# Turning w1 as raw fp32, reading lower_bound as rows, one chunk per turn and a new order of two scans in a tuned HGRN + maxout kernel

## The chip, the cores and the metric

The kernel runs on one core of one Trainium2 chip. The metric is the device time of one execution in microseconds (us); lower is better. Times quoted as "median" are medians over several executions. The profile is one execution recorded by the hardware; its "span" is some 2 us shorter than the timed number of the same execution. Engines are written PE (matmul), PEld (its weight loads), DVE (vector), ACT (scalar), POOL (GpSimd) and SP (the engine that issues most DMAs).

## The reference

```python
def _attn_ref(x, f_logit, lower_bound):          # x, f_logit: [4, 6144, 256] fp32
    f = lower_bound + (1 - lower_bound) * sigmoid(f_logit)
    h = 0
    for t in range(S):
        h = f[:, t] * h + (1 - f[:, t]) * x[:, t]
        y[:, t] = h
    return y

def _moe_ref(x, w1, w2, w_out):                  # x = y as [24576, 256]; w1, w2: [256, 1024]
    return np.maximum(x @ w1, x @ w2) @ w_out    # w_out: [1024, 256]
```

The kernel writes max(h1, h2) as h1 + relu(h2 - h1). With om = 1 - lower_bound it scans y without its factor om and puts om on the weights instead: `wd` = om·(w2 - w1) gives h2 - h1 in one product (the *first layer*), and `w13` = om·(w1 @ w_out) carries h1 straight to the output. For `w13`, w1 has to be turned (transposed) on PE. The *second layer* adds relu(h2 - h1) @ w_out and y @ `w13`.

## The kernel before

Tokens come in blocks of 512. Block 0 is loaded in two halves, cast to fp16 and turned by PE, so that work can start early; blocks 1 to 3 come as three chunks of one block. Chunks of 1024 tokens (from chunk 4 on) *cross*: POOL's DMA writes them as fp16 into a scratch in HBM, and a transposing DMA brings them back turned. From block 4 on the kernel works in pairs of blocks; a pair has 16 *slots*, each with two 128x512 matmuls of the first layer and 8 or 9 128x128 matmuls of a scheme that does the second layer of the pair before with seven products instead of eight. That scheme needs sums of quarters (`sum1` to `sum4`, tiles `S`), which DVE makes, beside the recurrences (`scan00`, `scan01`, `scan10`, `scan11` of a pair: first or second block, first or second half of the channels).

The head, with the weights, before the change:

```python
    NG = 2
    NQ = FC // NG                                   # 4
    ...
    def fetch_w(g):                                 # halves of w1 and w2 in turn, 512 KB each
        cols = slice(g * DFF // NG, (g + 1) * DFF // NG)
        for w, src in ((w1n, moe_w1), (w2n, moe_w2)):
            nc.sync.dma_start(out=w[g][:], in_=src[:, cols].rearrange("(kc p) f -> p kc f", p=P))
    def scale_w1(g):  # ACT: w1s = om * w1n, fp32
    def half_w1(g, copy):  # w1h = fp16 of w1s
    def turn_w1(g):
        pt = ps_o.tile([P, NQ, KC, P], HALF, name="ps")
        for q in range(NQ):
            for kc in range(KC):
                nc.tensor.transpose(pt[:, q, kc, :], w1h[g][:, kc, q : NQ * P : NQ], ident[:])
        return pt
    ...
        nc.scalar.dma_start(out=lbc[:], in_=lower_bound.rearrange("(h p) -> p h", p=P))
        fetch_first(0); fetch_first(1)              # f and x of block 0, two halves
        for g in range(NG):
            fetch_w(g)
        pool_waits(w1n[0][:, 0, 0:1])
        nc.gpsimd.dma_start(out=wob...)             # w_out
        for c in range(1, 6):
            for s in range(2):
                fetch(c, s)
        ...
        for q in range(24):                         # warm PE
            nc.tensor.transpose(wt[:, 0, 0:P], ident[:], ident[:])
        scale_w1(0); half_w1(0, nc.scalar.copy); scale_w1(1)
        pt0 = turn_w1(0)
        for pair in range(2):
            make_wd(0, pair)
            for fc in range(2 * pair, 2 * pair + 2):
                first_layer(0, fc)
        half_w1(1, nc.vector.tensor_copy)
        pt1 = turn_w1(1)
        for pair in range(2):
            make_wd(1, pair)
            for fc in range(4 + 2 * pair, 6 + 2 * pair):
                first_layer(0, fc)
        keep_w1T(0, pt0); keep_w1T(1, pt1)
        steps = turn_steps(1)
        make_w13(0)                                 # first product with w_out
        turn(steps[:8])                             # block 1: needs fT of chunk 1
        ...
        cross(4, 5)
```

The loop over pairs, with DVE's work placed by a position in the pair (nine positions to a slot):

```python
            seq = [
                (27, scans[p]["scan10"]),
                (36, scans[p]["scan11"]),
                (112, lambda: sum3(p)),
            ]
            if more:
                seq += [(64, decay0), (66, drive0), (70, scan00), (84, scan01),   # of pair p + 1
                        (131, decay1), (133, drive1)]
            if not first:
                seq += [(9, sum1 of p - 1), (18, sum2 of p - 1), (50, sum4 of p - 1)]
            ...
                if slot == 2 and p + 3 < NPAIR:
                    cross(blocks[2 * p + 6][3])
```

(Lines are joined and cut for reading.)

## Time and profile before

| | before |
|---|---|
| median time, 3 runs | 379.66 us (379.19 to 379.68) |
| span of the profiled run | 377.7 us |
| first matmul of the first layer | 11.48 us |
| first `w13` product (needs w_out) | 15.68 us |
| last first-layer matmul | 362.88 us |

The lines of the page that matter are the span, the busy times, and the shares of the chain that ended last:

```profile
span 377.7 us, 9593 instructions
...
PE 367.9 (97%) x4136; PEld 279.8 (74%) x4136; DVE 338.7 (90%) x410; ACT 302.4 (80%) x410; POOL 35.6 (9%) x79
...
PE 94%; DVE 3%; DMA 1%; issue 0%; SPq 0%; ACT 0%; DVEq 0%
```

PE is busy 97% of the span and is 94% of the chain. A kernel like this can change in time only where PE waits, where PE runs work that it need not run, or where PE starts late. The view of waits has one line per pair of waiter and releaser; after the colon stand the total in us, the number of waits and the longest. These are two of the waits of PE:

```profile
PE ps L137 <- DVE nat L128: 2.8, 2, 2.1
...
PE dT L441 <- DVE r L230: 0.2, 1, 0.2
```

The first is in the head, where PE waits for the casts of block 0's halves. The second is the only wait between 11.5 and 370 us: 0.24 us at 62 us, for a scan.

For the comparison I cut both executions at the same five PE instructions: the first first-layer matmul, the first matmul of block 1's first layer, the first-layer matmul that follows PE's first six matmuls on a tile `S` (pair 3, near 60 us), and the last first-layer matmul. The columns are the stretch, its length, busy us and instructions of PE, PEld, DVE, ACT and POOL, the granted PE clock, the DMA share and GB/s:

```profile
0.00:11.48 11.48, 6.68 (x56) 5.38 (x56) 6.46 (x17) 6.80 (x11) 3.92 (x12) 1.00 0.81 276
11.48:22.62 11.14, 11.14 (x102) 8.48 (x103) 8.89 (x17) 7.75 (x11) 3.39 (x7) 1.00 1.22 234
22.62:58.62 36.00, 36.00 (x264) 25.47 (x263) 29.10 (x45) 27.34 (x33) 2.48 (x6) 1.00 0.93 201
58.62:362.88 304.26, 304.02 (x3551) 231.01 (x3549) 287.33 (x326) 255.78 (x349) 25.78 (x55) 1.00 0.99 204
362.88:377.70 14.82, 10.04 (x169) 9.48 (x167) 6.93 (x8) 4.69 (x8) 0.00 (x0) 0.95 0.41 143
```

From 11.48 to 58.62 us PE's busy time equals the stretch: it is full. (The column of the clock reads 1.00 in the first stretch too; it doesn't show that PE runs slowly until the trace's throttle record grants the full clock, at 11.0 us.) The timeline has a line per group of like instructions: start, busy us, engine, source line, operation and tiles, and in brackets the idle time before and what ended it. Five groups of the head:

```profile
4.22 0.43 DVE L128 CAST nat<-osb 128x512 f16<-128x512 f32 x1 [2.66 <-DMA osb<-in_f_logit_dram]
...
7.94 2.77 PE L696 MATMUL dT<-ident 128*128 128x128 f16 x24
...
10.50 0.86 PE L383 MATMUL ps<-ident,S 128*128 128x128 f16 x8
...
10.97 1.65 DVE L365 SCALAR_TENSOR_TENSOR wd<-r,om 128x256 f16<-128x256 f32 x4
...
11.48 2.10 PE L441 MATMUL dT<-r,wd 128*128 128x512 f16 x8
```

f of block 0 is cast at 4.22 us; 24 warming transposes fill PE from 7.94 us at 107 ns each while the recurrence of block 0 runs; eight fp16 turns of w1 follow, `wd` is made from 10.97 us, and the first layer starts at 11.48 us. In pair 3's first slots DVE's order is this:

```profile
56.68 1.48 DVE L506 TENSOR_TENSOR S<-r 128x2560 f16<-128x2560 f16 x1
...
58.08 1.48 DVE L506 TENSOR_TENSOR S<-r,S 128x2560 f16<-128x2560 f16 x1
...
58.29 0.50 PE L650 MATMUL ps<-t,S 128*128 128x128 f16 x6
...
59.48 2.45 DVE L230 TENSOR_TENSOR_SCAN r<-ff,r,v 128x512 f16<-128x512 f16 x2
...
61.99 0.38 PE L441 MATMUL dT<-r,wd 128*128 128x512 f16 x1 [0.24 <-DVE r L230]
```

`sum1` (the 1.48 us at 56.68) ends at 58.16 us, 0.13 us before PE's first six matmuls on it (58.29). `sum2` follows, then both scans of the second block in one group, and the wait of 0.24 us at the end is the first layer's, for those scans.

### The profile page before, as it was taken

The page shows a single profiled execution, that of the slowest core. Times are in us where ns is not written, and L with a number is a line of the kernel's source. Part 1 is how long each engine was busy: PE and PEld are TensorE (multiplying, and loading weights), DVE is VectorE, ACT ScalarE, POOL GpSimd, SP SyncE. Part 2 cuts the span into 40 slices and gives each one's busy share as a digit, 9 for nine tenths or more (in the row PEclk, how much of TensorE's full clock was granted, in tenths as well). Part 3 has the DMA queues.
Part 4 walks back from the last instruction along what each step waited for, and adds up shares of the span by engine and source line. Part 5 has one row for each costly group of instructions (what it writes and reads, how often), then busy time and mean ns, then how long its engine had stood idle before and what let it go on. Part 6 is the DMA issues. An engine that isn't in the chain of part 4 may idle for free.

```text
span 377.7 us, 9593 instructions
## 1 busy us (share of the span) xinstructions
PE 367.9 (97%) x4136; PEld 279.8 (74%) x4136; DVE 338.7 (90%) x410; ACT 302.4 (80%) x410; POOL 35.6 (9%) x79
## 2 busy tenths in 40 slices
PE   5999999999999999999999999999999999999994
PEld 3777767777777777777777777777777777777784
DVE  4796789999999999999999999999999999999772
ACT  5865897888888798888888887887988888889752
POOL 1500101110101101101201201011011001010000
PEclk9999999999999999999999999999999999999999
DMA  7996979998999999999999899999899899980223
GB/s 254 246 223 131 309 143 214 227 193 189 273 134 257 223 184 266 222 184 225 203 200 301 208 161 254 147 247 274 132 263 279 134 241 221 185 282 3 112 113 114
DMA packets 104813, 77.17 MB, mean 204 GB/s; under 512 B 93570, under 2 KB 95618, under 8 KB 104066
## 3 DMA queue, kind: packets, MB, share of 16 engines
q1 hardware_dynamic: 101538, 51.19, 60.5%
q0 software_dynamic: 2544, 25.17, 34.7%
q8 instruction: 32, 0.52, 0.6%
q10 hardware_dynamic: 688, 0.20, 0.2%
q14 instruction: 11, 0.09, 0.1%
HBM read 53.48 MB, written 48.23 MB: 269 GB/s over the span
## 4 chain that ended last, share of the span: by engine, by line
PE 94%; DVE 3%; DMA 1%; issue 0%; SPq 0%; ACT 0%; DVEq 0%
PE ps L650 44%; PE dT L441 43%; PE ps L487 5%; DMA osb<-in_x_dram 1%; DVE S L506 1%; PE ps L180 1%; DVE r L230 1%; DVE r L264 1%; PE ps L397 0%; DVE v L223 0%; DVE osb L568 0%; DVE osb L496 0%; PE ps L137 0%; DVE osb L589 0%; PE ps L383 0%
## 5 line engine op out<-in xcount | busy, mean ns | idle before, releaser
L449 ACT ACTIVATE r<-dT 128x1024 f16<-128x1024 f32 x192 | 195.9, 1023 | 53.4 <-PE dT L441 53.2
L441 PE MATMUL dT<-r,wd 128*128 128x512 f16 x768 | 225.5, 379 | 0.4 <-DVE r L230 0.2
L650 PEld LDWEIGHTS <-S 128*128 128x128 f16 x1760 | 115.5, 101 | 37.6 <-issue 0.5
L650 PEld LDWEIGHTS <-r 128*128 128x128 f16 x1320 | 90.9, 101 | 36.8 <-issue 0.2
L230 DVE TENSOR_TENSOR_SCAN r<-ff,r,v 128x512 f16<-128x512 f16 x88 | 108.2, 1269 | 0.8
L650 PE MATMUL ps<-t,S 128*128 128x128 f16 x1320 | 101.6, 219 | 0.0
L506 DVE TENSOR_TENSOR S<-r 128x2560 f16<-128x2560 f16 x44 | 65.3, 1485 | 14.5 <-ACT r L449 14.4
L441 PEld LDWEIGHTS <-wd 128*128 128x128 f16 x768 | 67.6, 113 | 5.2 <-DVE wd L365 1.2
L650 PE MATMUL ps<-wob,r 128*128 128x128 f16 x704 | 69.9, 219 | 0.0
L506 DVE TENSOR_TENSOR S<-r,S 128x2560 f16<-128x2560 f16 x44 | 64.8, 1473 | 0.0
L285 ACT ACTIVATE u<-fT 128x512 f16<-128x512 f16 x88 | 56.0, 637 | 1.3 <-DMA fT<-scr 1.3
L213 DVE TENSOR_SCALAR ff<-u,nom 128x512 f16<-128x512 f16 (+1 forms) x98 | 31.5, 344 | 8.5 <-ACT u L285 3.7
L650 PE MATMUL ps<-w,r 128*128 128x128 f16 x176 | 38.5, 219 | 0.0
L348 POOL CAST waited<-fT 128x1 f32<-128x1 f16 x21 | 8.8, 418 | 282.8 <-DMA fT<-scr 282.8
L650 PE MATMUL ps<-t,r 128*128 128x128 f16 x430 | 34.1, 219 | 0.1
L568 DVE TENSOR_TENSOR osb<-ps,sn 128x512 f32<-128x512 f32 x44 | 30.1, 683 | 3.2 <-PE ps L650 3.2
L650 PE MATMUL ps<-wob,S 128*128 128x128 f16 x352 | 32.6, 219 | 0.0
L223 DVE TENSOR_TENSOR v<-u,xT 128x1024 f16<-128x1024 f16 x44 | 30.0, 682 | 0.0
L556 ACT COPY sn<-ps 128x512 f32<-128x512 f32 x44 | 25.8, 587 | 2.4 <-PE ps L650 2.4
L566 ACT COPY osb<-ps 128x512 f32<-128x512 f32 x43 | 25.0, 582 | 0.8 <-PE ps L650 0.8
L487 PEld LDWEIGHTS <-r 128*128 128x128 f16 x160 | 16.0, 101 | 6.6
L650 PE MATMUL ps<-w,S 128*128 128x128 f16 x88 | 19.3, 219 | 0.0
(58 smaller groups left out, 131.9 us busy)
## 6 DMA issues: line engine op xcount, KB each, us to landing
out_dram<-osb SPq DMA_DIRECT2D x46, 512.0 KB, 3.8
scr<-in_f_logit_dram POOLq DMA_DIRECT2D x22, 512.0 KB, 7.9
scr<-in_x_dram POOLq DMA_DIRECT2D x22, 512.0 KB, 10.5
r<-in_moe_w_dram SPq DMA_DIRECT2D x4, 512.0 KB, 6.9
fT<-in_f_logit_dram POOLq DMA_DIRECT2D x3, 256.0 KB, 7.9
xT<-in_x_dram POOLq DMA_DIRECT2D x3, 256.0 KB, 8.5
out_dram<-osb SPq DMA_DIRECT2D x3, 256.0 KB, 2.6
osb<-in_f_logit_dram SPq DMA_DIRECT2D x2, 256.0 KB, 4.5
```

The lines of the kernel that those rows point to most:

```text
L213: nc.vector.tensor_scalar(out=ff[:, h, cols], in0=u[:, h, cols], scalar1=nom[:, h : h + 1], scalar2=1.0, op0=ALU.mult, op1=ALU.add,)
L223: nc.vector.tensor_tensor(out=like(v[:, :, cols], xT), in0=like(u[:, :, cols], xT), in1=xT, op=ALU.mult,)
L230: nc.vector.tensor_tensor_scan(out=y_of(j, h), data0=ff[:, h, o : o + TB], data1=v[:, h, o : o + TB], initial=0.0 if t0 == 0 else y_of(j - ...
L285: nc.scalar.activation(out=mids[p + NBLK, "u"][:, h, cols], in_=held[c, 0][:, h, cols], func=AF.Sigmoid, scale=-1.0,)
L441: nc.tensor.matmul(dT[:, fc % 2, :], lhsT=wd[:, kc, unit_cols(fc)], rhs=y_of(j, kc), start=(kc == 0), stop=(kc == KC - 1),)
L449: nc.scalar.activation(out=rts[j, k][:, g - 1 : g + 1, :].rearrange("p q (i m) -> p q i m", m=P), in_=dT[:].rearrange("p q (m i) -> p q i ...
L487: nc.tensor.matmul(ps[:, r, :], lhsT=left, rhs=right, start=(s == 0 and r == 0), stop=(s == n - 1 and r == 1), skip_group_check=True,)
L506: nc.vector.tensor_tensor(out=t[:], in0=a, in1=b, op=op)
L556: nc.scalar.copy(out=t[:], in_=bank[b][:])
L566: nc.scalar.copy(out=dst, in_=bank[b][:])
L568: nc.vector.tensor_tensor(out=dst, in0=bank[b][:], in1=snap[name][:], op=ALU.add)
L650: nc.tensor.matmul(bank[b][:, i, :], lhsT=a[:, k, cols], rhs=w, start=fresh, stop=after is not None, skip_group_check=True,)
```

## The change

The intent has four parts. (1) lower_bound is read as two contiguous rows and turned by PE, not as 256 separate values. (2) w1 is fetched whole before w2 and turned raw, in fp32, as it lands; its scale om goes on `w13` at the end, so the fp16 casts of w1 vanish and all turns stand ahead of the first layer. w2 comes in quarters. (3) Chunks cross one at a time, so chunk 4 no longer waits for chunk 5; in the loop a chunk is then asked for two pairs ahead instead of three. (4) In pairs 2 and 3 some scans and gates move ahead of the sums. The core of the diff:

```diff
-    def cross(*cs):
-        if len(cs) > 1:
-            nc.sync.dma_start(out=seen[:], in_=scratch[1][cs[-1] % NSCR][CH - 1 : CH, 0:16])
-        for c in cs:
+    def cross(c):
             ...
-    NG = 2
+    NG = 4
     def turn_w1(g):
-        pt = ps_o.tile([P, NQ, KC, P], HALF, name="ps")
+        pt = ps_o.tile([P, NQ, KC, P], FP32, name="ps")
         ...
-                    pt[:, q, kc, :], w1h[g][:, kc, q : NQ * P : NQ], ident[:]
+                    pt[:, q, kc, :], half_of(w1n, g)[:, kc, q : NQ * P : NQ], ident_f[:]
     def make_w13(kc):
-        nc.scalar.copy(out=w13[:, kc, :], in_=psw[:, 0, :])
+        nc.scalar.mul(w13[:, kc, :], psw[:, 0, :], om[:, kc : kc + 1])
     ...
-        nc.scalar.dma_start(out=lbc[:], in_=lower_bound.rearrange("(h p) -> p h", p=P))
+        nc.scalar.dma_start(out=lbr[:], in_=lower_bound.rearrange("(h p) -> h p", p=P))
+        for h in range(DFF // TB):
+            fetch_w(w1n[h], moe_w1, h * TB)
         for g in range(NG):
-            fetch_w(g)
+            fetch_w(w2n[g], moe_w2, g * NQ * P)
-        for c in range(1, 6):
+        for c in range(1, 5):
     ...
+        lbc = ps_d.tile([P, TB], FP32, name="dT")
+        nc.tensor.transpose(lbc[:, 0:KC], lbr[:], ident_f[0:KC, 0:KC])
     ...
-        for q in range(24):
-            nc.tensor.transpose(wt[:, 0, 0:P], ident[:], ident[:])
-        half_w1(0, nc.scalar.copy)          # ... and the rest of the old head, in halves
+        for g in range(NG):
+            for q in range(6):
+                nc.tensor.transpose(wt[:, 0, 0:P], ident[:], ident[:])
+            pts.append(turn_w1(g))
+        for g in range(NG):
+            make_wd(g)
+            for fc in range(NQ * g, NQ * (g + 1)):
+                first_layer(0, fc)
-        cross(4, 5)
+        cross(4)
     ...                                     # in the loop over pairs:
-                (27, scans[p]["scan10"]),
-                (36, scans[p]["scan11"]),
+                (12 if p == PAIR0 + 1 else 36, scans[p]["scan11"]),
+            if p != PAIR0 + 1:
+                seq.append((27, scans[p]["scan10"]))
+            if first:
+                seq.append((126, scans[p + 1]["scan10"]))
-                    (131, scans[p + 1]["decay1"]),
-                    (133, scans[p + 1]["drive1"]),
+                    (110 if first else 131, scans[p + 1]["decay1"]),
+                    (111 if first else 133, scans[p + 1]["drive1"]),
-            gates = {4: 0, 6: 1, 12: 2, 14: 3} if more else {}
+            gates = {4: 0, 6: 1, 10 if first else 12: 2, 12 if first else 14: 3}
-                if slot == 2 and p + 3 < NPAIR:
-                    cross(blocks[2 * p + 6][3])
+                if slot == 2 and p + 2 < NPAIR:
+                    cross(blocks[2 * p + 4][3])
```

Here PAIR0 is 2. So `scan10` of pair 3 runs at the end of pair 2, and `scan11` of pair 3 at position 12 of pair 3, between `sum1` (position 9) and `sum2` (18) of pair 2.

More of the change, by code (lines that the diff above doesn't have):

```diff
@@ L40 @@
     NSEV = 7 * 4 * 5
+    W13_ORDER = (0, 1, 4, 5, 6, 7, 2, 3)
     assert S % CH == 0
@@ L142, in first_turn @@
             raws[k, s] = dst[:].rearrange("p k i m -> p k m i")
-    def cross(*cs):
-        if len(cs) > 1:
-            nc.sync.dma_start(
-                out=seen[:], in_=scratch[1][cs[-1] % NSCR][CH - 1 : CH, 0:16]
-            )
-        for c in cs:
-            for s in range(2):
-                dst = inpool.tile([P, KC, CH], HALF, name=("fT", "xT")[s])
-                nc.sync.dma_start_transpose(out=dst[:], in_=scratch[s][c % NSCR][:])
-                held[c, s] = dst
-        pool_waits(held[cs[-1], 0][:, 0, 0:1])
-        if cs[-1] + 1 < NCHUNK:
-            for s in range(2):
-                fetch(cs[-1] + 1, s)
+    def cross(c):
+        for s in range(2):
+            dst = inpool.tile([P, KC, CH], HALF, name=("fT", "xT")[s])
+            nc.sync.dma_start_transpose(out=dst[:], in_=scratch[s][c % NSCR][:])
+            held[c, s] = dst
+        pool_waits(held[c, 0][:, 0, 0:1])
+        if c + 1 < NCHUNK:
+            for s in range(2):
+                fetch(c + 1, s)
     def turn_steps(j):
@@ L320 @@
     nom = const.tile([P, KC], FP32)
-    lbc = const.tile([P, KC], FP32)
-    seen = const.tile([1, 16], HALF)
+    lbr = const.tile([KC, P], FP32)
     waited = const.tile([P, 1], FP32)
@@ L331, with fetch_w, half_of, scale_w1 @@
     )
-    NG = 2
+    NG = 4
     NQ = FC // NG
     w2n = [rpool.tile([P, KC, NQ * P], FP32, name="r") for g in range(NG)]
-    w1n = [rpool.tile([P, KC, NQ * P], FP32, name="r") for g in range(NG)]
-    w1s = [rpool.tile([P, KC, NQ * P], FP32, name="r") for g in range(NG)]
-    w1h = [spool.tile([P, KC, NQ * P], HALF, name="S") for g in range(NG)]
-    def fetch_w(g):
-        cols = slice(g * DFF // NG, (g + 1) * DFF // NG)
-        for w, src in ((w1n, moe_w1), (w2n, moe_w2)):
-            nc.sync.dma_start(
-                out=w[g][:],
-                in_=src[:, cols].rearrange("(kc p) f -> p kc f", p=P),
-            )
+    w1n = [rpool.tile([P, KC, TB], FP32, name="r") for h in range(DFF // TB)]
+    w1s = [rpool.tile([P, KC, TB], FP32, name="r") for h in range(DFF // TB)]
+    def fetch_w(tile_, src, first):
+        nc.sync.dma_start(
+            out=tile_[:],
+            in_=src[:, first : first + tile_.shape[-1]].rearrange(
+                "(kc p) f -> p kc f", p=P
+            ),
+        )
+    def half_of(w, g):
+        h, q = divmod(g, 2)
+        return w[h][:, :, q * NQ * P : (q + 1) * NQ * P]
     def pool_waits(t):
         nc.gpsimd.tensor_copy(out=waited[:], in_=t)
-    def scale_w1(g):
+    def scale_w1(h):
         for kc in range(KC):
-            nc.scalar.mul(w1s[g][:, kc, :], w1n[g][:, kc, :], om[:, kc : kc + 1])
-    def half_w1(g, copy):
-        for kc in range(KC):
-            copy(out=w1h[g][:, kc, :], in_=w1s[g][:, kc, :])
-    def make_wd(g, pair):
-        def cut(t):
-            return t.rearrange("p (n q) -> p n q", q=NQ)[:, :, 2 * pair : 2 * pair + 2]
+            nc.scalar.mul(w1s[h][:, kc, :], w1n[h][:, kc, :], om[:, kc : kc + 1])
+    def make_wd(g):
         for kc in range(KC):
             nc.vector.scalar_tensor_tensor(
-                out=cut(wd[:, kc, g * NQ * P : (g + 1) * NQ * P]),
-                in0=cut(w2n[g][:, kc, :]),
+                out=wd[:, kc, g * NQ * P : (g + 1) * NQ * P],
+                in0=w2n[g][:, kc, :],
                 scalar=om[:, kc : kc + 1],
-                in1=cut(w1s[g][:, kc, :]),
+                in1=half_of(w1s, g)[:, kc, :],
                 op0=ALU.mult,
@@ L383, in turn_w1, with keep_w1T @@
                 nc.tensor.transpose(
-                    pt[:, q, kc, :], w1h[g][:, kc, q : NQ * P : NQ], ident[:]
+                    pt[:, q, kc, :], half_of(w1n, g)[:, kc, q : NQ * P : NQ], ident_f[:]
                 )
         return pt
-    def keep_w1T(g, pt):
-        nc.vector.tensor_copy(
+    def keep_w1T(g, pt, copy):
+        copy(
             out=w1T[:, g * NQ : (g + 1) * NQ, :],
@@ L395, in make_w13 @@
         psw = ps_o.tile([P, 2, D], FP32, name="ps")
-        for fc in range(FC):
+        for n, fc in enumerate(W13_ORDER):
             nc.tensor.matmul(
@@ L400, in make_w13 @@
                 rhs=wob[:, fc, :],
-                start=(fc == 0),
-                stop=(fc == FC - 1),
+                start=(n == 0),
+                stop=(n == FC - 1),
             )
-        nc.scalar.copy(out=w13[:, kc, :], in_=psw[:, 0, :])
+        nc.scalar.mul(w13[:, kc, :], psw[:, 0, :], om[:, kc : kc + 1])
     lo, hi = slice(0, P), slice(P, 2 * P)
@@ L682 @@
             nc.tensor.transpose(wt[:, 0, 0:P], ident[:], ident[:])
+        lbc = ps_d.tile([P, TB], FP32, name="dT")
+        nc.tensor.transpose(lbc[:, 0:KC], lbr[:], ident_f[0:KC, 0:KC])
         first_bf16(0, 0, nc.vector.tensor_copy)
+        nc.vector.tensor_scalar_add(out=nom[:], in0=lbc[:, 0:KC], scalar1=-1.0)
+        nc.vector.tensor_scalar(
+            out=om[:], in0=lbc[:, 0:KC], scalar1=-1.0, scalar2=1.0, op0=ALU.mult,
+            op1=ALU.add,
+        )
         first_bf16(0, 1, nc.vector.tensor_copy)
-        nc.vector.tensor_scalar_add(out=nom[:], in0=lbc[:], scalar1=-1.0)
-        nc.vector.tensor_scalar(
-            out=om[:], in0=lbc[:], scalar1=-1.0, scalar2=1.0, op0=ALU.mult, op1=ALU.add
-        )
         first_turn(0)
@@ L694 @@
         first_recurrence(1)
-        for q in range(24):
-            nc.tensor.transpose(wt[:, 0, 0:P], ident[:], ident[:])
         scale_w1(0)
-        half_w1(0, nc.scalar.copy)
         scale_w1(1)
-        pt0 = turn_w1(0)
-        for pair in range(2):
-            make_wd(0, pair)
-            for fc in range(2 * pair, 2 * pair + 2):
-                first_layer(0, fc)
-        half_w1(1, nc.vector.tensor_copy)
-        pt1 = turn_w1(1)
-        for pair in range(2):
-            make_wd(1, pair)
-            for fc in range(4 + 2 * pair, 6 + 2 * pair):
-                first_layer(0, fc)
-        keep_w1T(0, pt0)
-        keep_w1T(1, pt1)
+        pts = []
+        for g in range(NG):
+            for q in range(6):
+                nc.tensor.transpose(wt[:, 0, 0:P], ident[:], ident[:])
+            pts.append(turn_w1(g))
+        keep_w1T(0, pts[0], nc.scalar.copy)
+        for g in range(NG):
+            make_wd(g)
+            for fc in range(NQ * g, NQ * (g + 1)):
+                first_layer(0, fc)
+        for g in (2, 3, 1):
+            keep_w1T(g, pts[g], nc.vector.tensor_copy)
         steps = turn_steps(1)
@@ L746 @@
                 early[fc]()
-        cross(6)
+        cross(5)
         scans = {PAIR0: pair_scans(PAIR0)}
@@ L769 @@
             more = p + 1 < NPAIR
+            if more:
+                scans[p + 1] = pair_scans(p + 1)
             seq = [
-                (27, scans[p]["scan10"]),
-                (36, scans[p]["scan11"]),
+                (12 if p == PAIR0 + 1 else 36, scans[p]["scan11"]),
                 (112, lambda: sum3(p)),
             ]
+            if p != PAIR0 + 1:
+                seq.append((27, scans[p]["scan10"]))
+            if first:
+                seq.append((126, scans[p + 1]["scan10"]))
             if more:
-                scans[p + 1] = pair_scans(p + 1)
                 seq += [
@@ L803 @@
                         queue.pop(0)()
-                if slot == 2 and p + 3 < NPAIR:
-                    cross(blocks[2 * p + 6][3])
-                if slot in gates:
+                if slot == 2 and p + 2 < NPAIR:
+                    cross(blocks[2 * p + 4][3])
+                if more and slot in gates:
                     pair_gate(p + 1, gates[slot])
```

## The prediction

> **What bounds the kernel now.** PE. The page gives PE 97% of the 377.7 us span; the chain that ended last is 94% PE. The waits view has PE waiting 4.8 us, nearly all before 7 us; the windows view shows PE busy without a hole from 11.5 to 370 us except 0.24 us at 62 us (a first-layer matmul waiting for the DVE scan). In steady state a slot is two 128x512 and 8 or 9 128x128 matmuls, 0.88 or 0.93 us in the timeline: nothing to gain. So three things can change the time: when dense first-layer matmuls start (11.48 us), the PE work and gaps from there to the end of the first w13 product (16.5 us), and the 0.24 us. The tail is untouched.
>
> **What the change does at the head.**
> 1. lower_bound. The trace's DMA packets show it as 272 packets of about 4 bytes, from 2.6 to 4.1 us. Meanwhile the queue carrying f, x and weights falls from 75-95 KB to 18-20 KB per 0.25 us; summed, some 440 KB, or 1.1 us at its full 385 KB/us. The Trainium skill (DMA: Bandwidth & Descriptors, Rules for kernel authors) says that a strided last dimension becomes one descriptor per element; 272 packets agree. Two contiguous rows remove it, so f (consumed at 4.22 us), x (5.53), second f (6.19) and w1 (8.26) should land about 1 us earlier.
> 2. The chain f, cast, transposes, sigmoid, DVE recurrences 0 and 1 (ends 11.05) follows by 1.0-1.2 us, so the first wd could be ready near 10.3.
> 3. w1 turn. 16 fp16 transposes of scaled w1 (8 of them, 0.45 us, between first-layer matmuls) become 16 fp32 ones of raw w1, all ahead of the first layer, with the same 24 warming ones (2.6 us at 108 ns) between. PE is free near 7.1, so it ends at 9.7 plus 16 fp32 transposes; at 108 ns (estimate: the cold fp16 rate) at 11.4. So I expect PE's own turns, not wd, to set the start of the first layer, at 10.8-11.5: most of the 1.1 us is eaten. The skill (TensorE: Matmul & The Clock Gate, Terms) says transpose mode is 4x faster for fp32; no run here shows it yet. At a fourfold price the start slips past 13 us and the change loses 2 us.
> 4. After the start, PE no longer waits for each wd (0.49 us of weight-load waits) and the casts of w1 vanish, but two dT buffers and ACT evictions (1.02 us each) still pace the first eight units: I count 0.3 us.
> 5. w2 in quarters after w1: the first quarter lands after 1.25 MB instead of 1 MB of weights; hidden.
>
> **In the middle.** Chunk 4 no longer waits for chunk 5 (that wait held SP 27.7 us, until 32.6). ACT's 1.3 us idle at 37.9 waiting for fT should go, and with it probably PE's 0.24 us. The later lead of two pairs instead of three is still more than a pair (about 14 us) against 5.7 us per crossing: no stall.
>
> **Sum.** 0.1-0.7 at the start, 0.3 in the first layer, 0.2 in the middle: about -0.8 us, 379.66 -> 378.9 us; 80% range 377.9 to 380.3. Faster by over 2%: 1%; within 2%: 98%; slower: 1%.
>
> **What would show it.** lower_bound as a few packets; f consumed near 3.2 us; y of block 0 finished near 10; first wd matmul at 10.8-11.5 with PE turning w1 until then; steady slots unchanged; no PE wait at 62 us.
>
> **What would make it wrong.** fp32 transposes of 200 ns or more (slower), or much cheaper, or an early warm clock (then up to -1.5 us); the clock's full grant (11.0 us before) coming later; a new DVE wait in pairs 2 and 3, whose scans are reordered.

## The result, and the profile after

The changed kernel gives a correct result and takes 381.36 us (median of 4, 381.1 to 381.5) against 379.67 us (4 runs, 379.19 to 379.68) of the kernel before in the same rounds. The ratio is 1.0047, 95% interval 1.0029 to 1.0064: within 2%, but slower, and outside the predicted range of 377.9 to 380.3. Ratios here and below are the mean time of one kernel's fast runs over that of the other's of the same rounds, so not quite the ratio of the medians.

```profile
span 379.7 us, 9601 instructions
...
PE 369.6 (97%) x4137; PEld 275.0 (72%) x4137; DVE 339.1 (89%) x409; ACT 302.1 (80%) x409; POOL 39.6 (10%) x80
...
PE 91%; DVE 4%; ACT 2%; DMA 1%; issue 0%; SPq 0%; DVEq 0%; ACTq 0%
```

PE is busy 1.7 us longer, and ACT and DVE have taken 3% of the chain from PE. The waits of PE show new lines:

```profile
PE ps L138 <- ACT nat L129: 1.6, 1, 1.6
...
PE ps L640 <- DVE S L496: 1.0, 2, 0.6
PE dT L431 <- ACT r L439: 0.2, 1, 0.2
```

The wait of the first layer for a scan is gone, as predicted. In its place stand 1.0 us of waits for `S`, a tile of sums made by DVE; before, PE never waited for one. The stretches cut at the same PE instructions:

```profile
0.00:13.11 13.11, 8.73 (x65) 7.51 (x66) 8.61 (x22) 6.98 (x11) 5.40 (x15) 1.00 0.91 271
13.11:24.04 10.93, 10.63 (x96) 7.89 (x94) 6.77 (x11) 7.08 (x9) 0.49 (x1) 1.00 1.25 243
24.04:60.73 36.69, 36.13 (x264) 24.23 (x262) 30.38 (x46) 28.17 (x34) 3.94 (x8) 1.00 0.95 199
60.73:365.19 304.46, 304.04 (x3552) 225.89 (x3550) 286.42 (x325) 255.22 (x348) 29.74 (x57) 1.00 0.99 202
365.19:379.70 14.51, 10.04 (x169) 9.48 (x167) 6.93 (x8) 4.69 (x8) 0.00 (x0) 0.92 0.42 146
```

| stretch, up to | before, us | after, us | difference |
|---|---|---|---|
| first first-layer matmul | 11.48 | 13.11 | +1.63 |
| block 1's first layer | 11.14 | 10.93 | -0.21 |
| behind the first six matmuls on `S`, pair 3 | 36.00 | 36.69 | +0.69 |
| last first-layer matmul | 304.26 | 304.46 | +0.20 |
| end | 14.82 | 14.51 | -0.31 |
| sum | 377.70 | 379.70 | +2.00 |

So the loss sits in two places: the start of the first layer, and about 0.9 us (0.69 + 0.20) around 60 us, where the steady part begins; the cut at 60.73 us falls between the two waits for `S`, and the stretch behind it has the second of them in place of the old 0.24 us. The 0.31 us at the end is the last store, which landed 4.0 us after DVE's last instruction and not 4.3; nothing in the change touches it. The timed medians differ by 1.7 us, not 2.0; the profiled run of the changed kernel was its slowest of four.

The head after:

```profile
3.43 0.43 DVE L129 CAST nat<-osb 128x512 f16<-128x512 f32 x1 [1.87 <-DMA osb<-in_f_logit_dram]
...
7.83 0.84 PE L695 MATMUL dT<-ident 128*128 128x128 f16 x6
...
8.47 1.06 PE L373 MATMUL ps<-ident_f,r 128*128 128x128 f32 x4
...
10.45 3.23 DVE L355 SCALAR_TENSOR_TENSOR wd<-r,om 128x256 f16<-128x256 f32 x8
...
12.58 0.69 PE L373 MATMUL ps<-ident_f,r 128*128 128x128 f32 x4
...
13.11 1.89 PE L431 MATMUL dT<-r,wd 128*128 128x512 f16 x8
```

f is now cast at 3.43 us, 0.79 us earlier. But the queue of warming transposes and fp32 turns starts at 7.83 us, hardly earlier than the warming before, and runs to 13.0 us without a wait; `wd` is made from 10.45 us and waits for nobody. A group of four fp32 turns takes 1.06 us at 8.47 and 0.69 us at 12.58: start to start, one is 213 ns before the clock is granted (12.17 us in the throttle record) and 110 to 120 ns after. An fp16 warming transpose is 107 ns and then 56 ns. Those two fp16 numbers are what the Trainium skill (TensorE: Matmul & The Clock Gate, Part 1) gives for a cold and a warm array at 128 columns, and the trace agrees. The queue adds up: 7.83 + 18 × 0.107 + 6 × 0.056 + 12 × 0.213 + 4 × 0.120 = 13.1 us, against the 13.11 us of the trace.

The clock has a part in this. The grant came at 12.17 us here and at 11.00 before, and it moves from execution to execution: over the seventeen profiles it came between 9.41 and 13.20 us. With the grant of before, the queue would have ended about 0.5 us sooner (an estimate from the four spacings above). In the seven variants that kept the old turns and did not hold the weights back, the first layer started between 11.18 and 11.70 us, though the grant came anywhere from 9.65 to 12.31; in the changed kernel PE's own queue sets the start, so the grant counts.

Around 60 us DVE's order is now this:

```profile
57.07 1.28 DVE L226 TENSOR_TENSOR_SCAN r<-ff,r,v 128x512 f16<-128x512 f16 x1
...
58.85 1.48 DVE L496 TENSOR_TENSOR S<-r 128x2560 f16<-128x2560 f16 x1
...
60.25 1.27 DVE L226 TENSOR_TENSOR_SCAN r<-ff,r,v 128x512 f16<-128x512 f16 x1
...
60.39 0.51 PE L640 MATMUL ps<-t,S 128*128 128x128 f16 x6 [0.56 <-DVE S L496]
...
61.44 2.99 DVE L496 TENSOR_TENSOR S<-r,S 128x2560 f16<-128x2560 f16 x2
...
62.97 0.34 PE L640 MATMUL ps<-t,S 128*128 128x128 f16 x3 [0.42 <-DVE S L496]
```

`scan10` of pair 3 (57.07) now stands before `sum1` (58.85, ends 60.33), and PE waits 0.56 us for it at 60.39. `scan11` (60.25) stands between `sum1` and `sum2`, which starts only at 61.44, and PE waits 0.42 us more at 62.97.

### The profile page after: what moved, and what is told of

Same layout as the page of the kernel before. It is cut to its first block, busy times and chain, and to the rows that moved or that the text cites. A ratio compares the mean times of both kernels' runs of the same rounds, so it can differ in the third digit from the quotient of the medians.

```text
span 379.7 us, 9601 instructions
## 1 busy us (share of the span) xinstructions
PE 369.6 (97%) x4137; PEld 275.0 (72%) x4137; DVE 339.1 (89%) x409; ACT 302.1 (80%) x409; POOL 39.6 (10%) x80
## 4 chain that ended last, share of the span: by engine, by line
PE 91%; DVE 4%; ACT 2%; DMA 1%; issue 0%; SPq 0%; DVEq 0%; ACTq 0%
PE ps L640 44%; PE dT L431 41%; PE ps L477 4%; DVE r L226 1%; DMA osb<-in_x_dram 1%; DVE S L496 1%; ACT r L439 1%; PE ps L373 1%; PE dT L695 1%; PE ps L176 0%; SPq L118 0%; DVE v L219 0%; DVE osb L486 0%; ACT u L281 0%; DVE ff L209 0%
## 5 line engine op out<-in xcount | busy, mean ns | idle before, releaser
L431 PEld LDWEIGHTS <-wd 128*128 128x128 f16 x768 | 61.1, 98 | 6.3 <-DVE w1T L379 0.5
L347 POOL CAST waited<-fT 128x1 f32<-128x1 f16 x22 | 14.0, 636 | 287.5 <-DMA fT<-scr 287.5
```

The costliest lines, as they stand in the source:

```text
L431: nc.tensor.matmul(dT[:, fc % 2, :], lhsT=wd[:, kc, unit_cols(fc)], rhs=y_of(j, kc), start=(kc == 0), stop=(kc == KC - 1),)
```

## The experiments

Fifteen variants ran. I write "shift" for the time at which PE reaches a given instruction, minus the time in the profile of the kernel before; the first mark is block 1's first layer (at 22.62 us before), the second the last first-layer matmul. A time to land is that of the last of a load's 16 completion increments.

### The order of the scans in pairs 2 and 3

**The changed kernel with the old order.** All of the change but part 4:

```diff
-                (12 if p == PAIR0 + 1 else 36, scans[p]["scan11"]),
+                (27, scans[p]["scan10"]),
+                (36, scans[p]["scan11"]),
-            if p != PAIR0 + 1:
-                seq.append((27, scans[p]["scan10"]))
-            if first:
-                seq.append((126, scans[p + 1]["scan10"]))
    ...   # decay1, drive1 and the gates back too
```

> The changed kernel with the old order of the vector engine's steps in pairs 2 and 3 (scan10 of pair 3 no longer drawn ahead of sum1, gates and decay1 back at their old slots); all else as changed. Theory A: the drawn-ahead scan10 (1.28 us) delays sum1, for which PE waits 0.56 and 0.42 us in pair 2; undoing it gives back 0.7 to 0.9 us: about 380.5 us, and no PE wait for an S tile. Rival: the waits come from the one-chunk crossing (later inputs, other DMA traffic), the order is neutral: 381.3 us, the waits stay or move to the scans (the old 0.24 us stall).

It took 380.96 us against 379.81, ratio 1.0024 (1.0003 to 1.0044). No wait for `S` was left, the old 0.2 us wait for the scan came back, and the shift did not grow in the middle: +1.99 at the first mark, +1.95 at the second. So the order made the second loss. (In this run the second half of f landed late, at 6.70 us, and the first layer started at 13.68; the head varies from run to run, which matters below.)

**The kernel before with one chunk per turn and the new order.** A rival was that the waits for `S` come only with the late head. This puts parts 3 and 4 on the old head:

```diff
-        cross(4, 5)
+        cross(4)
    ...   # and cross(5), and p + 2 in the loop, fetch(1 to 4)
+                (12 if p == PAIR0 + 1 else 36, scans[p]["scan11"]),
    ...   # the new order as in the change
```

> The kernel before with the one-chunk crossing and the new order of the vector engine's steps in pairs 2 and 3, its head untouched. Theory A: the order alone costs: PE waits about 1.0 us for S tiles in pair 2 and the shift against before grows by 0.7 to 0.9 us there: 380.3 us. Rival: the order costs only when the head is late, as in the changed kernel (start 13.1 us); with the head of before it is free and removes the 0.24 us wait: 379.4 us.

```profile
PE ps L644 <- DVE S L500: 1.0, 2, 0.6
PE ps L391 <- DMA wob<-in_moe_w_out_dram: 0.5, 1, 0.5
```

The two waits for `S` are there, 1.0 us, with the old head as well, and the shift grows by 0.89 us between the marks (+1.01 to +1.90). The rival falls. Ratio 1.0022 (1.0002 to 1.0042). The second line of the fence is a new surprise: PE waited 0.5 us for w_out, with a head that was not changed; the last share of w_out landed at 16.28 us, against 14.58 before.

**Each scan alone, and the gates alone.** Three variants of the run above:

```diff
 f1: scan11 of pair 3 at 12, scan10 back at 27
 f2: scan10 of pair 3 at 126 of pair 2, scan11 back at 36
 f3: only decay1, drive1 and the gates of pair 3 early
```

> Kernel before, one-chunk crossing, decay and drive of pair 3 early, and of the two scans only scan11 drawn ahead of sum2; scan10 behind sum2 as before. Theory A: PE's first wait (0.56 us, for sum1 behind scan10) is gone; the second (for sum2, behind scan11) stays with 0.4 to 1.2 us, since in the old order sum2 came just in time. Rival: both waits come of the early decay and drive: both stay, 0.9 us.

> The same, with only scan10 drawn ahead of sum1 and scan11 at its old place behind sum2. Theory A: a wait of about 0.6 us for sum1 stays, and sum2, which follows it at once, is then in time or nearly so: shift in pair 2 of 0.4 to 0.7 us, and the old 0.24 us wait for the scans goes, since only one scan is left before pair 3's first layer needs it. Rival: as above, both waits stay, 0.9 us.

> The same, with only the decay, drive and gates of pair 3 drawn ahead and both scans at their old place. Theory A: free: shift in pair 2 within 0.1 us, the old 0.24 us wait stays. Rival: the early decay and drive (1.3 us ahead of sum3) are what delays the sums: PE waits for S tiles, 0.4 to 0.9 us.

The timeline of the first, with `scan11` alone ahead:

```profile
57.76 1.28 DVE L225 TENSOR_TENSOR_SCAN r<-ff,r,v 128x512 f16<-128x512 f16 x1
...
58.95 1.47 DVE L500 TENSOR_TENSOR S<-r,S 128x2560 f16<-128x2560 f16 x1
...
60.48 0.34 PE L644 MATMUL ps<-t,S 128*128 128x128 f16 x3 [0.37 <-DVE S L500]
```

PE waits 0.37 us, for `sum2`, which starts behind the scan; from the first mark to 69 us the shift grows by 0.21 us. The timeline of the second, with `scan10` alone ahead:

```profile
55.62 1.27 DVE L225 TENSOR_TENSOR_SCAN r<-ff,r,v 128x512 f16<-128x512 f16 x1
...
57.40 1.48 DVE L500 TENSOR_TENSOR S<-r 128x2560 f16<-128x2560 f16 x1
...
58.94 0.51 PE L644 MATMUL ps<-t,S 128*128 128x128 f16 x6 [0.56 <-DVE S L500]
```

PE waits 0.56 us, for `sum1`; the net loss over the same stretch is 0.29 us, since the old 0.24 us wait for the scan is gone. With the gates alone the stretch loses nothing. Each scan thus puts its own wait in, through the sum just behind it. The two nets, 0.50 us, fall short of 0.89 by 0.39. Of this 0.24 us is the old wait, which each variant by itself also removes and which can be removed only once; 0.15 us stays unexplained. The whole times, 379.95, 379.92 and 380.04 us against 379.27, differ too little to rank (ratios 1.0018, 1.0017 and 1.0020, two runs each). (The first of the three lost another 0.8 us near 340 us, for a reason told under the next heading.)

### One chunk per turn

**The kernel before with part 3 alone:**

```diff
-        cross(4, 5)
+        cross(4)
...
-        cross(6)
+        cross(5)
```

> The kernel before with only the one-chunk crossing throughout (order of the steps in pairs 2 and 3 as before). Theory: neutral or slightly better, 379.4 to 379.7 us: PE is saturated there; chunk 4 arrives earlier so ACT's 1.3 us idle before its gate goes, PE's 0.24 us wait may go. Rival: the shorter lead or the changed DMA traffic starves pairs 2 and 3, and costs the 0.9 us that the changed kernel lost there: 380.5 us.

It took 379.64 us against 379.81, ratio 1.0001 (0.9978 to 1.0024), with shifts of 0.0 at both marks. In this profile it costs nothing and brings nothing: the 0.2 us wait for the scan stayed. So it was the order, not the crossing, that removed that wait in the changed kernel.

But the crossing has lost its slack. From the landing of a chunk's f to its first use (chunks 5 to 25) it was 6.4 us in the median and 2.5 at the least in the kernel before; it is 3.3 and 0.55 here, and 3.3 and 1.1 in the changed kernel. In the variant with `scan11` alone ahead, which also has one chunk per turn, three chunks came late:

```profile
340.67 0.63 ACT L280 ACTIVATE u<-fT 128x512 f16<-128x512 f16 x1 [1.44 <-DMA fT<-scr]
...
342.26 0.59 PE L435 MATMUL dT<-r,wd 128*128 128x512 f16 x2 [0.61 <-ACT r L443]
```

ACT waited for fT, its next eviction came late, PE waited 0.61 us for that, and the shift grew by 0.8 us. So part 3 is neutral only while no chunk comes late. The interval above leaves room for a cost of up to 0.9 us, and two of this variant's six runs took 380.9 us, which no profile explains.

### The turns of w1

**The changed kernel without the 24 warming transposes:**

```diff
         for g in range(NG):
-            for q in range(6):
-                nc.tensor.transpose(wt[:, 0, 0:P], ident[:], ident[:])
             pts.append(turn_w1(g))
```

> The changed kernel without the 24 warming transposes between the fp32 turns of w1. Theory B: PE's own queue (24 warming at 108 ns and 16 fp32 turns at 213 ns, from 7.8 to 13.0 us) sets the start of the first layer (13.11 us), not wd (first ready near 10.9) nor the weights' landing. Then the start moves to about 11.8 (16 x 213 ns after 8.4) and the time to about 380.1 us. Rival: the start is set by data (w2, wd, w1 landing): no change, 381.3. Second rival: without warming the clock is granted later and the first layer runs at half rate: start near 11.8 but less than 0.7 us gained.

```profile
8.36 3.02 PE L373 MATMUL ps<-ident_f,r 128*128 128x128 f32 x16
...
11.21 2.03 PE L431 MATMUL dT<-r,wd 128*128 128x512 f16 x8
...
15.93 1.03 PE L387 MATMUL ps<-wob,w1T 128*128 128x256 f16 x8 [0.51 <-DMA wob<-in_moe_w_out_dram]
...
17.24 0.62 PE L176 MATMUL ps<-ident,fT 128*128 128x128 f16 x8 [0.28 <-DMA fT<-in_f_logit_dram]
```

The sixteen turns alone take 3.02 us and run right up to the start of the first layer, at 11.21 us (their ends are modelled and overlap it), 1.9 us before the changed kernel's start. PE's own queue set the start. (The clock was granted at 10.48 us here, so the last turns took 110 to 120 ns.) But the gain is not kept: PE then waits 0.51 us for w_out at 15.93 and 0.28 us for fT of chunk 1 at 17.24, and the shift at the first mark is +0.77; the new order's waits for `S` follow as in the changed kernel. The median was 381.14 us against 379.81, ratio 1.0031 (1.001 to 1.0051).

This run tells something else. The throttle record grants the full clock at 10.48 us, when PE had run transposes only; the first ordinary matmul came at 11.21.

**Half of the turns** (a wrong result: half of w1 turned twice over; with the old order):

```diff
-            pts.append(turn_w1(g))
+            pts.append(turn_w1(g) if g < 2 else pts[g - 2])
```

> A diagnostic with a wrong result on purpose: the changed kernel with the old order in pairs 2 and 3, and only 8 of the 16 fp32 turns (their products used twice), all 24 warming transposes kept. It costs what 16 fp32 turns would cost at the 108 ns that the prediction assumed. Theory B: the start of the first layer falls by 8 x 213 ns = 1.7 us, to 11.4 or up to 12.0 when the second half of f lands late; that is, with the assumed price the predicted start would have held. Rival: the start is set by wd or the weights: it stays near 13.1 to 13.7.

The first layer started at 12.28 us, not at the 11.4 to 12.0 expected (PE also waited for w1), 1.40 us before that of the same kernel with all turns (whose second half of f had landed late) and 0.83 before that of the changed kernel. The median was 379.17 us against 379.55, ratio 0.9993 (0.9976 to 1.0011), where all turns gave 1.0024: the difference of the ratios is about 1.2 us, with intervals that leave about 1 us to either side. (In the profiled run w1 and w_out landed late, at 8.87 and 16.57 us, and it took 380.64; the others took 378.63 to 379.38.) By the starts, eight fp32 turns are worth 0.8 to 1.4 us here; the times agree, but are too wide to say it alone.

### lower_bound as rows

**The kernel before with part 1 alone:**

```diff
-        nc.scalar.dma_start(out=lbc[:], in_=lower_bound.rearrange("(h p) -> p h", p=P))
+        nc.scalar.dma_start(out=lbr[:], in_=lower_bound.rearrange("(h p) -> h p", p=P))
...
+        nc.tensor.transpose(lbc[:, 0:KC], lbr[:], ident_f[0:KC, 0:KC])
```

> The kernel before with only lower_bound read as two rows and turned by PE. Theory C: f is consumed near 3.4 us instead of 4.2, but the second half of f still lands at about 6.1 (as it did in the changed kernel, 6.06), so ACT's casts, the warming row on PE and wd start as before: 379.5 us, within 0.2 of before. Rival: the slow landing of the second half of f in the changed kernel was chance or came of the changed weight fetches; then it lands near 5.1 and the time falls by 0.5 to 1.0 us, to 378.7 to 379.2.

f landed early, at 3.49 us, but its second half landed at 6.79 us (6.17 before), and the first layer started at 11.70. Ratio 0.9993 (0.9968 to 1.0018): nothing gained. The load itself did what was predicted: 272 packets from 2.7 to 4.0 us became 4 packets at about 1.7 us (the rule on strided last dimensions that the prediction names agrees with this). Yet over all profiles the early start is spent before the second half of f lands. Eight profiles have columns and eight have rows (the one with held weights, told next, is in neither). The mean landing of the last share is:

| | f, first half | f, second half | w1, first half |
|---|---|---|---|
| columns (8) | 4.27 us | 6.12 us | 8.21 us |
| rows (8) | 3.40 us | 6.06 us | 8.47 us |

In the changed kernel the queue falls to 30 to 66 KB per 0.25 us between 4.25 and 5.5 us, with single packets of 250 to 900 ns among the usual ones of 84, and the last of the sixteen shares of f's second half comes at 6.06 us where fifteen are there at 5.08. That a load counts as done only with its last of up to 16 independent shares is what the Trainium skill says (DMA: Bandwidth & Descriptors, Why a DMA increments its semaphore by 16 and not by 1), and the 16 increments of the trace agree.

**Rows, with the weights held back** until the second half of f has landed (a diagnostic, not meant to win):

```diff
+        nc.sync.dma_start(out=held_back[:], in_=raws[1, 0][0:1, 0, 0:16])
         for g in range(NG):
             fetch_w(g)
```

> A diagnostic, slower on purpose: the kernel before with lower_bound as rows, and the weights' loads held until the second half of f has landed. Theory D: the slow packets between 3.6 and 5.5 us, and the one straggling share of the second half of f (landing 6.1 to 6.8 instead of 5.1), come of the weights' loads being issued or fetched then; with them held, the second half of f lands at 4.6 to 5.1 in all its shares. Rival: the slow spell comes whatever is in flight; it still lands at 6 or later. The time is about 381 to 382 us either way.

The second half of f now landed at 5.30 us, with all its shares together, while the kernel lost (382.77 us against 379.67, ratio 1.0078; its trace also shows the clock at half from 12.82 to 16.23 us). But two variants with rows and without holding, the next one and the last one below, also had it at 5.01 and 5.31 us. So the weights behind it don't by themselves make the slow spell; its cause stays open.

**The changed kernel without the new order and without warming, with rows and with columns.**

```diff
 e7: the old order as in e1, no warming transposes as in e2
 e8: the same, and lower_bound read as columns again
```

> The changed kernel without warming transposes and with the old order in pairs 2 and 3. From the two single undoings: start 11.2 us, then the wait for w_out as in the run without warming, shift +0.6 to +0.8 against before at the second layer, no S waits: about 380.3 us. Rival: the w_out wait was a chance of that run, then 379.3.

> As the run beside it, but lower_bound read as before (256 elements of 4 bytes). If the rows are what makes one share of the loads straggle, w_out lands near 14.6 to 14.9 as before, the first layer starts near 11.4 and the first w13 product near 15.2 (15.7 before): about 379.3 us, 0.3 to 0.4 below before and about 1 us below the run with rows. Rival: the rows are harmless; then this one is as fast as the run with rows.

With rows it took 379.45 us (ratio 0.9998, 0.9975 to 1.0021), with columns 380.18 us (1.0010, 0.9992 to 1.0028). The starts were 11.11 and 11.35 us. The shift at the first mark was +0.04 and +0.67, and the greater one has its w_out landing at 15.85 us, so the rows are not what makes w_out late. The two intervals overlap. The one with rows is the best of the correct variants with the new turns, and equal to the kernel before: the earlier start (0.37 us) was given back, with a wait of 0.3 us for fT of chunk 1.

### w_out

The last share of w_out landed at 14.58 us before and at 14.52 in the changed kernel, but at 15.15 to 16.57 us in eight of the eleven others that issue it behind the same loads, with heads of both kinds. When it comes after 16 us, PE waits 0.3 to 0.5 us for it and 0.2 to 0.3 us for fT, and the shift at the first mark is +1.0 to +1.2 even with the head of before (parts 3 and 4: 16.28 us, +1.01; the gates alone: 16.49 us, +1.22). Only the changed kernel with the old order had it at 16.07 us without a wait, since its late first layer asked for it only at 17.59. In the run with parts 3 and 4, fifteen of its sixteen shares had landed by 14.53 us and the last came at 16.28.

**w_out issued earlier**, in the changed kernel without order and warming, and in the kernel before:

```diff
-        pool_waits(w1n[0][:, 0, 0:1])
+        pool_waits(raws[1, 1][:, 0, 0:1])
```

> The changed kernel with the old order in pairs 2 and 3, no warming transposes, and w_out and the chunks of the second block asked for when the second half of x has landed instead of when the first half of w1 has. Theory E: with the turns out of the way the head is bound by the landing of w_out (14.6 to 16.1) and of chunk 1's f (0.3 us wait); asked for 1.3 to 1.7 us earlier, they stop being waited for: shift against before of -0.5 to -0.7 at the second layer, 378.9 us. Rival: they share the same engines with w2, so wd of the last quarters comes late and nothing is gained: 379.4.

> The kernel before with w_out asked for when the second half of x has landed. Its start (11.48) is set by the recurrence, wd and the cast of w1, and w_out lands 1.1 us before its use in the profiled run: no change in a good run (379.6), but the runs in which w_out straggles (one of the profiled runs had it at 16.3 and lost 1.0 us) should become rarer: a smaller spread. Rival: the second half of w1 and w2 land later and the start slips: 380 us.

In the first, the first layer started only at 12.36 us: w1 landed late, at 8.77 us, and as the clock was granted at 13.20 us all sixteen turns ran at 213 ns. Then `wd` waited 0.67 us for w2, until 13.95. The median of the five fast runs was 380.16 us against 379.55, ratio 1.0001 (0.9983 to 1.0019; one slow run of 384.86 us left out). In the second nothing was gained (379.77 us, ratio 1.0002, 0.999 to 1.0014). In neither did w_out land earlier (15.87 and 14.71 us), while the last share of w2 came at 13.92 and 13.52 us, where it was 11.99 in the changed kernel and 12.27 before. So asking for w_out sooner cost w2 time and did not bring w_out sooner.

**w_out earlier and half of the turns after the first units** (otherwise as the first of these two):

```diff
-        for g in range(NG):
+        for g in range(2):
             pts.append(turn_w1(g))
...
+            if g == 2:
+                pts += [turn_w1(2), turn_w1(3)]
```

> As e10, with the turns of the second half of w1 moved behind the fourth unit of the first layer, where PE waits for ACT anyway. If the turn queue sets the start (11.1 us with wd ready at 10.5), the start falls to about 10.5 and the time to about 378.6, unless the clock is not granted yet then (cold units take 0.43 us): 379.0. Rival: the bound is already DMA: as e10.

The first layer started at 10.99 us, the earliest of all, and still the first `w13` product came at 17.00 us: DVE's `wd` waited 1.10 and 1.31 us for quarters of w2, the last of which landed at 15.38 us; w_out landed at 15.21. The time was 381.06 us against 379.55, ratio 1.0040 (1.0028 to 1.0052). All three runs fit the rival, that w_out and w2 share what the DMA engines can bring; none measures that limit by itself.

## Why the prediction was wrong

The prediction was -0.8 us; the medians say +1.7 and the profiles +2.0. Its sum had three terms: 0.1 to 0.7 us gained at the start, 0.3 in the first layer and 0.2 in the middle.

- **The start (step 3) failed.** "16 fp32 transposes; at 108 ns (estimate: the cold fp16 rate)" was measured at 213 ns before the clock's grant and 110 to 120 ns after, twice the fp16 price at either clock. The whole chain of that step was right in kind: PE's own turns set the start, and not `wd` (the run without warming started 1.9 us earlier). The arithmetic of 11.4 against 13.11 us splits into three: the turns took 3.04 us (12 × 0.213 + 4 × 0.120) where 1.73 were counted (+1.31); the queue began at 7.83 us where 7.1 was counted (+0.73); the warming took 2.26 us where 2.6 were counted, as its last six ran at the granted clock (-0.34). The price per turn is the mis-sized term; 200 ns or more stood among the things that would make the prediction wrong. The error was to take the fp16 rate, the only one that the trace of before showed, as the middle of the estimate. How many turns fall before the grant varies from execution to execution: at the grant of before the loss would have been some 0.5 us smaller (the estimate above). A later grant stood among the listed risks too, and it came in the profile.
- **The early data (steps 1 and 2) failed in part.** The 256 small packets vanished, and f was cast 0.79 us earlier: right. "Second f and w1 should land about 1 us earlier" was wrong: 0.1 to 0.2 us in this pair of profiles, and in the mean of eight each f's second half came 0.06 us earlier and w1 0.26 us later, for a cause that stays open. y of block 0 was ready 0.5 us earlier and not 1.0 to 1.2.
- **After the start (step 4)** 0.34 us were won back by the sixth unit of the first layer, of which 0.21 were left at block 1's, as against 0.3 predicted: about right. w2's quarters stayed hidden (step 5): right.
- **The middle failed.** The 0.24 us wait went, as predicted, but the crossing was not its cause: with the crossing alone it stayed. I counted the order of the scans as a risk in the last sentence and put no cost on it. It costs 0.89 us, shown with the new head (without it the shift stays at 1.95 to 1.99, with it it grows from 1.42 to 2.31) and with the old head (adding it, 0.89 again): `sum1` had 0.13 us to spare before, and a scan of 1.28 us was put ahead of it. No crossing came late in the changed kernel's profile and the steady part kept its pace (304.26 and 304.46 us): right, but with 1.1 us to spare at the least. The prediction set the lead against the 5.7 us of the transposing DMA alone; from the issue of a chunk's load to the landing of its f it is 13.4 us in the median before and 14.0 after. In one other run with one chunk per turn three chunks came late.
- **Not foreseen:** the head is within about 1 us of a second limit. Before, w_out landed 1.1 us ahead of its first use at 15.68 us. Each variant with the changed turns that started before 11.4 us (11.21, 11.11, 11.35 and 10.99 us) gave its lead back to waits for w_out, w2 or fT. So even turns at the price assumed would probably not have brought the whole predicted gain; no run shows this directly.

Two things stay open: what makes the queue slow from 4.25 us on once f comes early, and why w_out's last share is late in some executions. The second is spread over the executions of every variant, the kernel before included (379.03 to 381.86 us over the rounds), so no difference of a few tenths between variants is explained here by anything but waits seen in their traces.

## What to carry to other kernels

Before moving transposes from fp16 to fp32 to save casts, measure one fp32 transpose at the clock where it will run: here it cost twice the fp16 one, before the clock's grant and after, on the engine that set the start. Before moving an instruction ahead on a busy engine, read how much slack the next instruction's consumer has; here 0.13 us of slack met a scan of 1.28 us. Before shortening a lead, count the whole way of the data and not only its last step. A gain at the start of a kernel lasts only as far as the next load's landing, and that landing has to be read from more than one execution.

## What the Trainium skill lacked or had wrong

- TensorE: Matmul & The Clock Gate, Terms, says that transpose mode is four times faster for fp32, with no baseline; FP8 and Floating Point Precision, TensorE Precision Notes, says that a true fp32 product takes four passes. Read together they suggest one pass. The runs show two fp16 times: 213 ns against 107 before the clock's grant, 110 to 120 ns against 56 after. No page gives this price.
- TensorE: Matmul & The Clock Gate, Part 4, says that the full clock does not engage for transpose mode ("it doesn't count as PE-busy the same way"). In the run without warming the full clock was granted at 10.48 us with only transposes run so far and the first ordinary matmul at 11.21; in the kernel before, at 11.0 us against 11.48. (The profile lists these transposes as matmuls and does not show their mode.)
- DMA: Bandwidth & Descriptors does not say how far apart the shares of one load may land. w_out's last share came between 14.5 and 16.6 us over thirteen profiles that issue it behind the same loads, in one of them 1.7 us after the other fifteen.
